# A column of ones beside V, attention ahead of the fold, and 384 columns a matmul

## The chip, the cores and the metric

The kernel runs on one core of a Trainium2 chip. Its engines are TensorE (PE; PEld is its weight load), VectorE (DVE), ScalarE (ACT), GpSimd (POOL) and SyncE (SP, which here issues every DMA). Each has its own queue of instructions, in order. The metric is device time in microseconds (us) of one execution, as the median of several runs.

## What is computed

A random-feature attention, a gated layer with two products behind it, and four experts that all work on every token:

```
q, k, v: 2 batches x 8 heads x 576 tokens x 64
phi(x) = exp(x omega' - |x|^2/2 - max) / sqrt(128)        # 128 features a token
kv = k'^T v ;  z = sum over tokens of k'
attn = (q' kv) / (q' z + 1e-6)                            # per head
x = attn as 1152 tokens x 512
h = ((x w1) * (x w2)) w3 w_out                            # 512 -> 1024 -> 1024 -> 512
out = sum over e of p_e * relu(h ew1_e) ew2_e             # 4 experts, 512 -> 1024 -> 512
```

w1, w2, w3 and w_out come as float64, the rest as float32. Products after the attention are made of operands that are each the sum of two float32r numbers (a high and a low part, made by `split`), in three passes: low by high, high by low, high by high.

## The kernel before

**Tokens.** Each batch has 576 tokens, 512 main ones (4 x 128) and a tail of 64. The tails of both batches share one tile of 128 rows. A *pair* is two heads of one batch; there are eight pairs. x stands transposed in `xt`, with one set of four tiles for each batch.

**The attention of a pair** (lines 261 to 365). `load` fetches k, q and v of 512 tokens. `transpose_kq` turns k and q on TensorE. `features` (L215) makes 4 x 128 projections in one PSUM bank, VectorE takes their maximum (L227), ScalarE makes four exponentials (L229). `sum_k` adds K' over tokens on GpSimd (L298 to L300), `kv_sums` (L309) makes (K'V)^T of both heads at once, `kv_place` (L315 and L316) turns it back and spreads the sums of K' with a matmul of ones. `normalise` (L333 to L338) multiplies each row of Q' by the sums on VectorE, adds it up, inverts it, and GpSimd scales Q'. `transpose_e` (L348) turns Q' and `attend` (L363) makes 288 columns of x at a time. A pair is spread over three steps of a loop.

**Float64 weights.** `from_f64` (L75 to L86) loads a block of 128 x 512 numbers (512 KB) into one of two tiles and makes float32 of it with one ScalarE and three VectorE instructions (L83, L84, L85). `split` (L69, L70) then takes ScalarE for the high and, for w1, w2 and w_out, GpSimd for the low part. There are 48 such blocks: 16 of w1 and w2, of which 8 are converted a second time, 8 of w_out, 16 of w3.

**The middle.** `gated` makes 128 rows of (x w1) * (x w2) for one batch in two pieces of 288 columns (L147). `fold` makes w3 w_out: four transposes of a w3 block (into ps_w and ps_x by turns), a split, 12 matmuls of 512 columns (L174), twice for each of eight rows; the sums stand in ps_po and ps_et by turns. `expert_input` multiplies the two for one batch (L192).

**The experts.** For each, eight groups of first-layer columns in four pieces of 288 (L474) and nine token tiles of 512 columns (L493). Their raw weights go through `raw_p`, four tiles that exist from the start.

**The order.** A scheduler orders the instructions of each engine by priority. Table `BESIDE` says what stands beside each attention step (conversions and the first six gated rows of batch 0), `AFTER` what follows. Attention steps run with a priority shift of -100.

## Time and profile before

| | |
|---|---|
| median of 3 runs | 733.59 us (733.46 to 733.74) |
| the profiled execution, first to last instruction | 732.2 us |
| TensorE busy | 700.5 us, 96% |
| VectorE busy | 345.6 us, 47% |
| ScalarE busy | 241.0 us, 33% |
| GpSimd busy | 100.7 us, 14% |

The span leaves out some 1.4 us that lie around the first and last instruction. The page cuts the span into 40 slices; "busy" for TensorE means that some matmul is in flight, not that the engine is at its peak. Shares are averages over stages: the attention fills roughly the first 165 us, the fold follows to about 238, then the other products, and from 329 us on the experts run, 100.17 us each.

### The profile page before, as it was taken

Reading aid. Unit: us, or ns where it says so; the run is one execution under the profiler, and the core shown is the slowest. Engines: PE = TensorE matmul, PEld = TensorE weight load, DVE = VectorE, ACT = ScalarE, POOL = GpSimd, SP = SyncE. Lnnn points to the kernel's source line nnn. Section 1 sums busy time; section 2 is a strip of 40 time slices with the busy share of each in tenths; the row PEclk is TensorE's granted clock in tenths of the full one; section 3 lists DMA queues with packets and bytes.
Section 4 is the critical chain, followed back from the end, with each engine's and each line's share of the span. In section 5 each row is a group of like instructions: output and inputs, shape, how many; then the busy total and the mean of one; then the engine's idle time right before and its main releaser. Section 6 shows DMA issues by size and latency. Waiting matters only on the chain.

```text
span 732.2 us, 10963 instructions
## 1 busy us (share of the span) xinstructions
PE 700.5 (96%) x4353; PEld 625.6 (85%) x4353; DVE 345.6 (47%) x752; ACT 241.0 (33%) x602; POOL 100.7 (14%) x114
## 2 busy tenths in 40 slices
PE   6997887889999999999999999999999999999997
PEld 4765667778888999999998899988899988999886
DVE  3799999997766275612431154231334311422111
ACT  4777766464332254512330033210223200322000
POOL 1557664450000041000000000000000000000000
PEclk9999998999999999999999999999999999999999
DMA  6526322453443021500110031010211100100011
GB/s 175 174 77 198 116 86 88 144 173 126 133 144 116 1 87 44 162 26 2 58 59 0 1 116 56 3 58 0 71 46 59 59 1 0 58 1 1 30 49 52
DMA packets 37858, 52.13 MB, mean 71 GB/s; under 512 B 6960, under 2 KB 25392, under 8 KB 37808
## 3 DMA queue, kind: packets, MB, share of 16 engines
q1 hardware_dynamic: 37808, 51.44, 22.8%
q8 instruction: 34, 0.56, 0.3%
q14 instruction: 16, 0.13, 0.1%
HBM read 49.07 MB, written 2.36 MB: 70 GB/s over the span
## 4 chain that ended last, share of the span: by engine, by line
PE 80%; DVE 14%; DMA 2%; ACT 2%; issue 1%; SPq 0%; POOL 0%; DVEq 0%; ACTq 0%
PE ps_f L493 7%; PE ps_f L474 7%; PE ps_et L493 4%; PE ps_kv L493 4%; PE ps_t L474 3%; PE ps_w L474 3%; PE ps_kv L474 3%; PE ps_po L474 3%; PE ps_x L474 3%; PE ps_et L474 3%; PE ps_et L174 3%; DVE t L333 3%; PE ps_t L493 3%; PE ps_w L493 3%; PE ps_x L493 3%; PE ps_po L493 3%
## 5 line engine op out<-in xcount | busy, mean ns | idle before, releaser
L474 PE MATMUL ps_f<-x,w 128*128 128x288 f32 x384 | 102.7, 295 | 0.0
L474 PEld LDWEIGHTS ps_f<-x,w 128*128 128x128 f32 x384 | 72.3, 188 | 0.1
L69 ACT ACTIVATE w<-w2r 128x512 fp32r<-128x512 f32 x32 | 20.2, 632 | 140.1 <-PE ps_f L493 44.5
L147 PE MATMUL ps_w<-xt,w 128*128 128x288 f32 x240 | 49.3, 309 | 8.7 <-ACT a L154 3.4
L493 PE MATMUL ps_f<-w,hid 128*128 128x512 f32 x240 | 56.1, 389 | 0.0
L493 PEld LDWEIGHTS ps_f<-w,hid 128*128 128x128 f32 x240 | 44.9, 188 | 9.2
L147 PE MATMUL ps_po<-xt,w 128*128 128x288 f32 x240 | 48.5, 307 | 4.0 <-DVE a L158 3.1
L474 PE MATMUL ps_w<-x,w 128*128 128x288 f32 x192 | 51.4, 295 | 0.0
L474 PE MATMUL ps_t<-x,w 128*128 128x288 f32 x192 | 51.4, 295 | 0.0
L474 PE MATMUL ps_kv<-x,w 128*128 128x288 f32 x192 | 51.4, 295 | 0.0
L474 PE MATMUL ps_po<-x,w 128*128 128x288 f32 x192 | 51.4, 295 | 0.0
L474 PE MATMUL ps_x<-x,w 128*128 128x288 f32 x192 | 51.4, 295 | 0.0
L474 PE MATMUL ps_et<-x,w 128*128 128x288 f32 x192 | 51.3, 295 | 0.0
L70 POOL TENSOR_TENSOR w<-w12f,w 128x512 fp32r<-128x512 f32 x24 | 33.4, 1394 | 120.3 <-ACT w L69 112.9
L147 PEld LDWEIGHTS ps_w<-xt,w 128*128 128x128 f32 x240 | 38.7, 195 | 11.7 <-ACT a L154 3.7
L147 PEld LDWEIGHTS ps_po<-xt,w 128*128 128x128 f32 x240 | 38.7, 195 | 5.7 <-DVE a L158 3.6
L83 DVE TENSOR_SCALAR f64e<-f 128x512 uint32<-128x512 uint32 x48 | 27.0, 567 | 24.8 <-DMA f<-in_moe_w_dram 23.8
L84 DVE SCALAR_TENSOR_TENSOR f64e<-f,f64e 128x512 uint32<-128x512 uint32 x48 | 38.4, 803 | 0.5
L474 PEld LDWEIGHTS ps_kv<-x,w 128*128 128x128 f32 x192 | 36.2, 189 | 0.0
L474 PEld LDWEIGHTS ps_w<-x,w 128*128 128x128 f32 x192 | 36.2, 189 | 0.0
L474 PEld LDWEIGHTS ps_t<-x,w 128*128 128x128 f32 x192 | 36.2, 189 | 0.0
L474 PEld LDWEIGHTS ps_et<-x,w 128*128 128x128 f32 x192 | 36.1, 188 | 0.1
(194 smaller groups left out, 1472.2 us busy)
## 6 DMA issues: line engine op xcount, KB each, us to landing
f<-in_moe_w_dram SPq DMA_DIRECT2D x40, 512.0 KB, 3.7
w1r<-in_moe_w_dram SPq DMA_DIRECT2D x32, 256.0 KB, 3.0
w2r<-in_moe_w_dram SPq DMA_DIRECT2D x32, 256.0 KB, 2.8
f<-in_moe_w_out_dram SPq DMA_DIRECT2D x8, 512.0 KB, 3.6
kr<-in_k_dram SPq DMA_DIRECT2D x8, 256.0 KB, 2.8
vr<-in_v_dram SPq DMA_DIRECT2D x8, 256.0 KB, 3.7
qr<-in_q_dram SPq DMA_DIRECT2D x8, 256.0 KB, 2.8
out_dram<-acc SPq DMA_DIRECT2D x8, 256.0 KB, 2.1
```

The lines of the kernel that those rows point to most:

```text
L69: nc.scalar.activation(out=hi, in_=src, func=ACTF.Copy)
L70: (eng or nc.vector).tensor_tensor(out=lo, in0=src, in1=hi.bitcast(F32), op=ALU.subtract)
L83: nc.vector.tensor_scalar(out=e, in0=high, scalar1=0x80000000, scalar2=None, op0=ALU.bitwise_and)
L84: nc.vector.scalar_tensor_tensor(out=e, in0=low, scalar=29, in1=e, op0=ALU.logical_shift_right, op1=ALU.bitwise_or)
L147: nc.tensor.matmul(out=bs[c][:, :HS], lhsT=w12[w, g][:, x, kk], rhs=xt[b][kk][:, y, c * HS:(c + 1) * HS], start=(kk == 0 and n == 0), stop ...
L174: nc.tensor.matmul(out=po, lhsT=wt[:, a, g * P:(g + 1) * P], rhs=wo[hf * 4 + g][:, c], start=(n == 0), stop=(n == 3 * KF - 1),)
L333: nc.vector.scalar_tensor_tensor(out=t, in0=e[:, g], scalar=1.0, in1=zs[g], op0=ALU.mult, op1=ALU.mult, accum_out=d[:, g],)
L474: nc.tensor.matmul(out=banks[2 * b + c][:, :HS], lhsT=w1t[kk][:, x, g * P:(g + 1) * P], rhs=x2[b, kk][:, y, c * HS:(c + 1) * HS], start=(k ...
L493: nc.tensor.matmul(out=ps, lhsT=hd[f][:, x, t * P:(t + 1) * P], rhs=w2t[f][:, y], start=(n == 0), stop=(n == 3 * KE - 1),)
```

## The change

- V stands in tiles of 65 columns a head, `va`, with a column of ones at the end. The product K'V (L320 of the new kernel) then has the sums of K' as its 65th column, and Q' times that has the denominator beside the numerator. `normalised` inverts and multiplies 256 numbers a head, not Q'. `sum_k`, `kv_place` and `normalise` are gone. The product comes with tokens in rows, and `place` turns it.
- Q' is made by one subtraction of all four maxima on VectorE and one exponential (`wide`).
- The tails of Q' are turned once at the start, and `attend_tail` does the tails of a batch behind its last pair.
- A pair takes two steps. The attention has a priority shift of 100000. Beside it stand the conversion of w_out and the fold; the tables are gone. The fold has one bank for transposes and one for sums, and two w3T tiles.
- All low halves of converted weights are made by VectorE. Every block is converted once: 40 in all.
- `gated`, `expert_input` and the experts' first layer work on all 1152 tokens in three pieces of 384 columns (`columns`), over eight banks in turn.
- `raw_p` opens after the gated stage.

```diff
-BESIDE = {
-    3: "w0 w1", 4: "w2", 5: "b00 w3 o", 6: "b01 w4 o", 7: "b02 w5 o", 8: "b03 w6 o", 9: "b04 w7 b05 o",
-}
-AFTER = "b06 b07 o o o f0 f1 f2 f3 f4 f5 f6 f7 c0 b14 b15 b16 b17 w0 b10 w1 b11 w2 b12 w3 b13 c1"
...
+ATTENTION_FIRST = 100000
...
-    HS = S // 2
+    CH = NT // 3
...
-    xt_p = ctx.enter_context(tc.tile_pool(name="xt", bufs=2 * KD))
-    w1_p = ctx.enter_context(tc.tile_pool(name="w1", bufs=8))
-    raw_p = ctx.enter_context(tc.tile_pool(name="raw", bufs=4))
+    xt_p = ctx.enter_context(tc.tile_pool(name="xt", bufs=KD))
+    w1_p = ctx.enter_context(tc.tile_pool(name="w1", bufs=10))
...
+    def next_bank():
+        turn[0] += 1
+        return bank(("t", "f", "kv", "et", "f", "x", "w", "po")[turn[0] % 8])
...
-        f = cv.tile([P, 512], F32, tag="f64f", name=name, bufs=3)
+        f = cv.tile([P, 512], F32, tag="f64f", name=name, bufs=2)
...
-    xt = [[xt_p.tile([P, 2, S], F32R, tag="xt", name=f"xt{i}") for i in range(NPAIR)] for _ in range(B)]
...
+    xt = [xt_p.tile([P, 2, NT], F32R, tag="xt", name=f"xt{i}") for i in range(NPAIR)]
...
-    wo_p = mctx.enter_context(tc.tile_pool(name="wo", bufs=KF))
-    h_p = mctx.enter_context(tc.tile_pool(name="h", bufs=KF))
...
+    w3_p = mctx.enter_context(tc.tile_pool(name="w3", bufs=1))
...
-            t = load_w64(w1_p, src, "w12", nc.gpsimd)
...
-        wo.append(load_w64(wo_p, mwo[f * P:(f + 1) * P].unsqueeze(1), "wo", nc.gpsimd))
...
-    def fold(w3_p, m):
...
-        po = bank(("po", "et")[m % 2])
...
+            t = load_w64(w1_p, src[:, g * P:(g + 1) * P].rearrange("(k p) c -> p k c", p=P), "w12", nc.vector)
...
+        wo.append(load_w64(w1_p, mwo[f * P:(f + 1) * P].unsqueeze(1), "wo", nc.vector))
...
+    def fold(m):
...
+        po = bank("po")
...
-            ps = bank(("w", "x")[hf])
+            ps = bank("w")
...
-            wt = w3_p.tile([P, 2, 512], F32R, tag="w3T", name="w3T", bufs=3)
+            wt = w3_p.tile([P, 2, 512], F32R, tag="w3T", name="w3T", bufs=2)
...
+    def columns(lhsT, rhs, nk):
...
+        bs = [next_bank() for _ in range(NT // CH)]
+        for kk in range(nk):
+            for n, (x, y) in enumerate(PASSES):
+                for c, ps in enumerate(bs):
+                    nc.tensor.matmul(
+                        out=ps[:, :CH], lhsT=lhsT(kk, x), rhs=rhs[kk][:, y, c * CH:(c + 1) * CH],
+                        start=(kk == 0 and n == 0), stop=(kk == nk - 1 and n == 2),
+                    )
+        return [(ps[:, :CH], slice(c * CH, (c + 1) * CH)) for c, ps in enumerate(bs)]
...
+    def gated(a_p, h_p, g):
...
+        ws = load_w12(g)
+        ht = h_p.tile([P, 2, NT], F32R, tag="h", name="hid")
+        parts = []
+        for w in range(2):
+            for c, (ps, s) in enumerate(columns(lambda kk, x: ws[w][:, x, kk], xt, KD)):
+                if w == 0:
+                    t = a_p.tile([P, CH], F32, tag="a", name="a", bufs=6)
+                    nc.scalar.activation(out=t, in_=ps, func=ACTF.Copy)
+                    parts.append(t)
+                else:
+                    t = parts[c]
+                    nc.vector.tensor_tensor(out=t, in0=ps, in1=t, op=ALU.mult)
+                    split(ht[:, HI, s], ht[:, LO, s], t)
+        hid.append(ht)
...
+    def expert_input():
         for j in range(KD):
...
+            t = xt_p.tile([P, 2, NT], F32R, tag="xt", name="x2")
+            for ps, s in columns(lambda kk, x: w3o[kk][:, x, j * P:(j + 1) * P], hid, KF):
+                split(t[:, HI, s], t[:, LO, s], ps)
+            x2.append(t)
...
-            for g in range(4):
-                last = nc.scalar.activation(out=e[:, g], in_=pv[:, g], func=ACTF.Exp, bias=mx[:, g:g + 1])
+            if wide:
+                nc.vector.tensor_tensor(out=e, in0=pv, in1=mx.unsqueeze(2).to_broadcast([P, 4, M]), op=ALU.add)
+                last = nc.scalar.activation(out=e, in_=e, func=ACTF.Exp)
+            else:
+                for g in range(4):
+                    last = nc.scalar.activation(out=e[:, g], in_=pv[:, g], func=ACTF.Exp, bias=mx[:, g:g + 1])
...
+        va = [st.tile([P, 2 * R, D1], F32, name=f"va{n}") for n in range(3)]
+        for t in va:
+            nc.gpsimd.memset(t[:, :, D:], 1.0)
...
-        eqt = st.tile([P, H, M], F32, name="eqt")
+        eTt = st.tile([P, H, P], F32, name="eTt")
...
+            m, t = (0, MAIN) if b == 0 else (S + TAIL, S)
+            return slice(m, m + MAIN), slice(t, t + TAIL)
...
+        def normalised(out, ps, rows, n):
...
+            v = ps[rows, :n * D1].rearrange("p (n d) -> p n d", d=D1)
+            d = at.tile([P, 4], F32, tag="d", name="d", bufs=4)[rows, :n]
+            nc.vector.tensor_scalar(out=d, in0=v[:, :, D], scalar1=EPS, scalar2=None, op0=ALU.add)
+            nc.vector.reciprocal(out=d, in_=d)
+            nc.vector.tensor_tensor(
+                out=out, in0=v[:, :, :D], in1=d.unsqueeze(2).to_broadcast(list(out.shape)), op=ALU.mult,
+            )
...
+                self.va = va[self.n % 3]
...
-                for name, src, bufs in (("kr", k, 1), ("qr", q, 1), ("vr", v, 2)):
...
+                for h in range(2):
+                    nc.sync.dma_start(
+                        out=self.va[:, h * R:(h + 1) * R, :D], in_=v[b, 2 * i + h, :MAIN, :].rearrange("(p r) d -> p r d", r=R),
+                    )
...
+                self.eq[j] = at.tile([P, R, M], F32, tag="eq", name="eq", bufs=3)
+                self.mark = features(self.qT, j, self.eq[j], wide=True)
...
                 ps = bank("kv")
...
+                for j in range(2):
+                    h = 2 * self.i + j
+                    for r in range(R + 1):
+                        e, a = (self.ek[j][:, r], self.va[:, j * R + r]) if r < R else (ekt[:, h], vt[self.b][:, h])
+                        nc.tensor.matmul(out=ps[:, j * D1:(j + 1) * D1], lhsT=e, rhs=a, start=(r == 0), stop=(r == R))
+                self.kva = at.tile([P, 2, D1], F32, tag="kva", name="kva", bufs=NPAIR + 1)
+                nc.scalar.activation(out=self.kva, in_=ps[:, :2 * D1].rearrange("p (j d) -> p j d", j=2), func=ACTF.Copy)
...
+                self.eT[j] = at.tile([P, MAIN], F32, tag="eT", name="eT", bufs=2)
+                for r in range(R):
+                    transpose(ps[:, r * P:(r + 1) * P], self.eq[j][:, r])
+                nc.scalar.activation(out=self.eT[j], in_=ps, func=ACTF.Copy)
...
+            def attend(self):
+                self.xs = at.tile([P, R, 2, D], F32, tag="xs", name="xs")
+                for j in range(2):
+                    ps = bank(("x", "kv")[j])
                     for r in range(R):
...
+                        nc.tensor.matmul(
+                            out=ps[:, r * D1:(r + 1) * D1], lhsT=self.eT[j][:, r * P:(r + 1) * P], rhs=self.kva[:, j],
+                            start=True, stop=True,
                         )
...
+                    normalised(self.xs[:, :, j], ps, slice(0, P), R)
...
+            def place(self):
+                ps = bank("et")
+                for r in range(R):
+                    transpose(ps[:, r * P:(r + 1) * P], self.xs[:, r].rearrange("p j d -> p (j d)"))
+                x, s = xt[self.i], cols(self.b)[0]
+                split(x[:, HI, s], x[:, LO, s], ps)
...
+        def attend_tail(b, ps_of):
...
+            rows = rows_of[b]
+            xs = at.tile([P, H, D], F32, tag="xs", name="xs")
+            for f in range(2):
+                ps = bank(("x", "kv")[f])
+                for g in range(4):
+                    h = f * 4 + g
+                    nc.tensor.matmul(
+                        out=ps[rows, g * D1:(g + 1) * D1], lhsT=eTt[:, h, rows], rhs=ps_of[h // 2].kva[:, h % 2],
+                        start=True, stop=True,
+                    )
+                normalised(xs[rows, f * 4:(f + 1) * 4], ps, rows, 4)
...
-        for n in range(len(pairs) + 2):
-            u, u1, u2, nx = pair(n), pair(n - 1), pair(n - 2), pair(n + 1)
-            with tc.high_priority(offset=-100):
...
+        for n in range(len(pairs) + 1):
+            u, u1, nx = pair(n), pair(n - 1), pair(n + 1)
+            with tc.high_priority(offset=ATTENTION_FIRST):
...
-                if u:
-                    for j in range(2):
-                        u.features_k(j)
-                        u.sum_k(j)
                 if u1:
                     u1.kv_sums()
-                if u2:
-                    for j in range(3):
-                        u2.transpose_e(j)
+                if u:
+                    u.features_k(0)
+                    u.features_k(1)
+                if u1:
+                    u1.transpose_e(0)
+                    u1.transpose_e(1)
                 if u:
                     u.features_q(0)
+                    u.features_q(1)
                 if u1:
-                    u1.kv_place()
-                if u:
-                    u.features_q(1)
-                if u2:
-                    u2.attend(0)
-                    u2.attend(1)
-                if u1:
-                    for j in range(3):
-                        u1.normalise(j)
+                    u1.attend()
                 if nx:
                     nx.transpose_kq()
...
+                if u1:
+                    u1.place()
+                    if u1.i == NPAIR - 1:
+                        attend_tail(u1.b, pairs[u1.n - u1.i:u1.n + 1])
+        for f in range(KF):
+            load_wo(f)
+        for m in range(KF):
+            fold(m)
...
-    for s in AFTER.split():
...
+    h_p = mctx.enter_context(tc.tile_pool(name="h", bufs=KF, reuse_waits="tile"))
+    a_p = mctx.enter_context(tc.tile_pool(name="a", bufs=1, reuse_waits="tile"))
+    for g in range(KF):
+        gated(a_p, h_p, g)
+    expert_input()
...
+    raw_p = ctx.enter_context(tc.tile_pool(name="raw", bufs=4, reuse_waits="tile"))
...
+                for ps, s in columns(lambda kk, x: w1t[kk][:, x, g * P:(g + 1) * P], x2, KD):
+                    nc.scalar.activation(out=ht[:, HI, s], in_=ps, func=ACTF.Relu)
                     nc.vector.scalar_tensor_tensor(
-                        out=ht[:, LO, s], in0=banks[c][:, :HS], scalar=0.0, in1=ht[:, HI, s].bitcast(F32),
-                        op0=ALU.max, op1=ALU.subtract,
+                        out=ht[:, LO, s], in0=ps, scalar=0.0, in1=ht[:, HI, s].bitcast(F32), op0=ALU.max, op1=ALU.subtract,
                     )
```

How the queues move is seen at three places. First SP at the start, where `kr` and `qr` at L233 (L229 after) are the tails of k and q, and `va` is V. Before:

```order
L233 DMA kr<-in_k_dram 64x8x64 x2
L245 DMA om_raw<-in_omega_dram 128x64
L233 DMA qr<-in_q_dram 64x8x64 x2
L233 DMA vt_117<-in_v_dram 64x8x64
L233 DMA vt_120<-in_v_dram 64x8x64
L274 DMA kr<-in_k_dram 128x2x256
```

After:

```order
L298 DMA va_108<-in_v_dram 128x4x64
L298 DMA va_109<-in_v_dram 128x4x64 x2
L298 DMA va_108<-in_v_dram 128x4x64
L229 DMA kr<-in_k_dram 64x8x64 x2
L242 DMA om_raw<-in_omega_dram 128x64
L229 DMA qr<-in_q_dram 64x8x64 x2
L229 DMA vt_113<-in_v_dram 64x8x64
```

Four loads of V, of the second and third pair, moved ahead of the first tails.

Second VectorE in the middle of the attention. Before, about the third pair (`t,d<-eq,z` is the product with the sums of K'):

```order
L333 SCALAR_TENSOR_TENSOR t,d<-eq,z 128x128 x2
L85 SCALAR_TENSOR_TENSOR w12f<-w12f,f64e 128x512
L84 SCALAR_TENSOR_TENSOR f64e<-f_862,f64e 128x512
L333 SCALAR_TENSOR_TENSOR t,d<-eq,z 128x128
L227 TENSOR_REDUCE mx<-ps_f 128x4
L210 TENSOR_SCALAR kT<-ps_t 128x512
L333 SCALAR_TENSOR_TENSOR t,d<-eq,z 128x128
L70 TENSOR_TENSOR xt_84<-ps_x,xt_84 128x288
```

After, between two rounds of the fold (`w3T` is the split of the transposed w3 block, `w3f` and `f64e` belong to the conversion of the next blocks):

```order
L63 TENSOR_TENSOR w3T<-ps_w,w3T 128x512
L78 SCALAR_TENSOR_TENSOR w3f<-w3f,f64e 128x512
L219 TENSOR_REDUCE mx<-ps_f 128x4
L202 TENSOR_SCALAR kT<-ps_t 128x512
L76 TENSOR_SCALAR f64e<-f_1420 128x512
L77 SCALAR_TENSOR_TENSOR f64e<-f_1420,f64e 128x512
L63 TENSOR_TENSOR w3o<-ps_po,w3o 128x512
L63 TENSOR_TENSOR w3T<-ps_w,w3T 128x512
```

The products are gone, and the fold's conversions and splits stand in their place. In this order the first split w3T is VectorE's 81st row, the last its 232nd; the last piece of `xt` is written by its 296th.

Third TensorE near the end of the attention. Before, the last attention matmuls (L363) stand among gated ones of batch 0:

```order
L147 MATMUL ps_kv<-xt_84,w_1840 128x288
L147 MATMUL ps_t<-xt_85,w_1840 128x288
L363 MATMUL ps_x<-eT,kv 64x288 x2
L147 MATMUL ps_kv<-xt_85,w_1840 128x288
L147 MATMUL ps_t<-xt_85,w_1840 128x288
```

After, the K'V sums of the last pair (L320):

```order
L159 MATMUL ps_f<-xt_80,w_1732 128x384
L159 MATMUL ps_w<-xt_80,w_1732 128x384
L159 MATMUL ps_f<-xt_81,w_1732 128x384
L320 MATMUL ps_kv<-va_108,ek 128x65 x4
L320 MATMUL ps_kv<-vt_117,ekt 128x65
L320 MATMUL ps_kv<-va_108,ek 128x65 x4
L320 MATMUL ps_kv<-vt_117,ekt 128x65
L92 MATMUL ps_et<-ident,xs 128x128 x4
L159 MATMUL ps_f<-xt_81,w_1732 128x384 x2
```

Gated matmuls stand ahead of the last pair here too, 72 of the 576 before the last piece of x is placed.

## Rows read from the trace of the kernel before

**Rows 1.** The page: span, and busy time (share, instructions) by engine.

```profile
span 732.2 us, 10963 instructions
PE 700.5 (96%) x4353; PEld 625.6 (85%) x4353; DVE 345.6 (47%) x752; ACT 241.0 (33%) x602; POOL 100.7 (14%) x114
```

**Rows 2.** Stretches: busy us (x instructions) of five engines, clock, DMA share, GB/s.

```profile
0.00:10.00 10.00, 4.11 (x14) 3.41 (x15) 1.37 (x4) 1.88 (x2) 2.09 (x10) 1.00 0.61 151
10.00:20.00 10.00, 8.73 (x38) 6.66 (x37) 5.44 (x8) 7.17 (x25) 0.80 (x2) 1.00 0.74 196
...
30.00:165.00 135.00, 116.38 (x748) 90.77 (x746) 129.82 (x345) 88.99 (x249) 81.02 (x86) 0.97 0.41 126
```

**Rows 3.** The chain that ended last, in order of time: start, us, what.

```profile
316.09 3.20 PE ps_x L192 x24
...
378.81 5.47 PE ps_f L493 x24
384.28 5.44 PE ps_kv L493 x24
...
478.98 5.46 PE ps_kv L493 x24
...
728.33 0.75 DVE acc L501
```

**Rows 4.** VectorE by line (total, mean ns): three from 100 us, four from 165.

```profile
L85 DVE SCALAR_TENSOR_TENSOR wof<-wof,f64e 128x512 uint32<-128x512 uint32 x7 | 8.9, 1266 | 0.2
L333 DVE SCALAR_TENSOR_TENSOR t<-eq,z 128x128 bf16<-128x128 f32 x16 | 5.5, 375 | 0.0
L70 DVE TENSOR_TENSOR xt<-ps_x,xt 128x288 fp32r<-128x288 f32 x6 | 2.7, 448 | 0.0
...
L84 DVE SCALAR_TENSOR_TENSOR f64e<-f,f64e 128x512 uint32<-128x512 uint32 x19 | 13.1, 687 | 0.3
L85 DVE SCALAR_TENSOR_TENSOR w3f<-w3f,f64e 128x512 uint32<-128x512 uint32 x15 | 10.3, 684 | 0.1
L83 DVE TENSOR_SCALAR f64e<-f 128x512 uint32<-128x512 uint32 x19 | 8.1, 428 | 20.9 <-DMA f<-in_moe_w_dram 20.8
L70 DVE TENSOR_TENSOR w3T<-ps_w,w3T 128x512 fp32r<-128x512 f32 x8 | 5.5, 686 | 0.3 <-ACT w3T L69 0.3
```

**Rows 5.** VectorE in order of time: start, us, line, operation.

```profile
64.34 0.68 DVE L85 SCALAR_TENSOR_TENSOR w12f<-w12f,f64e 128x512 uint32<-128x512 uint32 x1
64.94 0.16 DVE L336 TENSOR_SCALAR d<-d 128x4 f32<-128x4 f32 x1
...
65.90 0.68 DVE L227 TENSOR_REDUCE mx<-ps_f 128x4 f32<-128x512 f32 x1
```

**Rows 6.** SP's queue at the start, in order of time.

```profile
0.74 1.44 SPq L233 DMA_DIRECT2D kr<-in_k_dram  x2
...
4.21 1.31 SPq L233 DMA_DIRECT2D vt<-in_v_dram  x2
```

**Rows 7.** The fold: chain, four transposes, both halves of a split.

```profile
183.24 3.04 PE ps_et L174 x12
...
188.17 2.74 PE ps_et L174 x12
191.47 2.75 PE ps_po L174 x12
...
126.56 0.66 PE L99 MATMUL ps_et<-ident,eq 128*128 128x128 f32 x4
...
186.75 0.60 ACT L69 ACTIVATE w3T<-ps_w 128x512 fp32r<-128x512 f32 x1 [2.51 <-PE ps_w L99]
...
187.38 0.69 DVE L70 TENSOR_TENSOR w3T<-ps_w,w3T 128x512 fp32r<-128x512 f32 x1 [0.26 <-ACT w3T L69]
```

**Rows 8.** A stretch, and TensorE in order of time, about 120 us.

```profile
120.00:130.00 10.00, 10.00 (x54) 9.34 (x55) 9.18 (x20) 7.37 (x17) 3.52 (x3) 0.71 0.52 159
...
119.97 3.25 PE L147 MATMUL ps_w<-xt,w 128*128 128x288 f32 x12 [3.44 <-ACT a L154]
```

More of the change, by code (lines that the diff above doesn't have):

```diff
@@ L127, in load_w12 @@
+    hid, wo, w3o, x2 = [], [], [], []
     def load_w12(g):
[L129 to L159 removed]
@@ L201, in attention_moe_kernel @@
         st = actx.enter_context(tc.tile_pool(name="st", bufs=1))
+        D1 = D + 1
         def transposed(r, name, tag="t"):
@@ L213, in transposed, with features @@
             return t
-        def features(t, half, e, tag="f"):
+        def features(t, half, e, tag="f", wide=False):
             ps = bank(tag)
@@ L358, in attend @@
-            def attend(self, c):
-                ps = bank("x")
-                s = slice(c * HS, (c + 1) * HS)
-                for j in range(2):
-                    h = slice(j * D, (j + 1) * D)
-                    nc.tensor.matmul(out=ps[h, :HS], lhsT=self.kv[:, h], rhs=self.eT[j][:, s], start=True, stop=True)
-                x = xt[self.b][self.i]
-                split(x[:, HI, s], x[:, LO, s], ps[:, :HS])
+                for j in range(2):
[3 more added lines that the diff above has]
+                        nc.tensor.matmul(out=ps[:, j * D1:(j + 1) * D1], lhsT=e, rhs=a, start=(r == 0), stop=(r == R))
@@ new lines, in place @@
+            def place(self):
+                ps = bank("et")
+                for r in range(R):
+                    transpose(ps[:, r * P:(r + 1) * P], self.xs[:, r].rearrange("p j d -> p (j d)"))
[11 more added lines that the diff above has]
+                        start=True, stop=True,
+                    )
+                normalised(xs[rows, f * 4:(f + 1) * 4], ps, rows, 4)
+            ps = bank("et")
+            s = cols(b)[1]
+            for i in range(NPAIR):
+                transpose(ps[:, i * TAIL:(i + 1) * TAIL], xs[rows, 2 * i:2 * i + 2].rearrange("p j d -> p (j d)"), rows)
+            for i in range(NPAIR):
+                x = xt[i]
+                split(x[:, HI, s], x[:, LO, s], ps[:, i * TAIL:(i + 1) * TAIL])
@@ L377, in attention_moe_kernel @@
         for half in range(2):
-            features(qT, half, eqt[:, half * 4:half * 4 + 4], ("w", "po")[half])
-        for n in range(len(pairs) + 2):
-            u, u1, u2, nx = pair(n), pair(n - 1), pair(n - 2), pair(n + 1)
-            with tc.high_priority(offset=-100):
+            e = at.tile([P, R, M], F32, tag="eq", name="eq", bufs=3)
+            features(qT, half, e, ("w", "po")[half])
+            ps = bank("x")
+            for g in range(4):
+                transpose(ps[:, g * P:(g + 1) * P], e[:, g])
@@ L401, in attention_moe_kernel @@
-                if u2:
-                    u2.attend(0)
-                    u2.attend(1)
-                if u1:
-                    for j in range(3):
-                        u1.normalise(j)
+                    u1.attend()
                 if nx:
                     nx.transpose_kq()
-            with ExitStack() as order:
-                for ins in u.mark if u else ():
-                    order.enter_context(tc.issue_after(ins))
-                for s in BESIDE.get(n, "").split():
-                    if s[0] == "w":
-                        load_w12(int(s[1]))
-                    elif s[0] == "o":
-                        load_wo()
-                    else:
-                        gated(at, 2, int(s[1]), int(s[2]), ("w", "po") * 2)
```

148 lines of the change are left out of this document (16 added, 132 removed).

## The prediction

> **What bounds the kernel now.** I read the page first. TensorE is busy for 700.5 of 732.2 us [rows 1], an average over stages: where it is full only its own work counts, elsewhere something else may set the pace. The cut into stretches shows where: from 30 to 165 us VectorE is busy for 129.8 of 135 us, TensorE for 116.4 and ScalarE for 89.0 [rows 2]. The attention stage is bound by VectorE. The first 20 us are a start-up in which VectorE works for 1.37 + 5.44 = 6.8 us, so it idles for 13.2 [rows 2].
>
> From about 170 us on the chain runs on TensorE alone. Its price per matmul is read from groups of 24: 3.20 us for 288 columns, 5.44 us for 512, that is 133.3 and 226.7 ns [rows 3]. The difference, 93.3 ns for 224 columns, is 0.4167 ns a column (2.4 GHz); what is left is 13.3 ns a matmul at either size. One expert takes 478.98 - 378.81 = 100.17 us: 384 matmuls of 288 (51.2) and 216 of 512 (48.97). VectorE takes the last sum at 728.33, and the span ends 3.9 us later.
>
> **Columns: 384 in place of 288.** The same columns go through in three pieces, not four. A matmul of 384 costs 160 + 13.3 = 173.3 ns. There are 672 matmuls fewer (192 in the gated product, 96 in the expert input, 384 in the experts' first layer), so 672 x 13.3 ns = 9.0 us leave a path that has nothing beside it. New stage times: gated 576 x 173.3 = 99.8 us (102.4 before), expert input 288 x 173.3 = 49.9 (51.2), four experts 4 x (49.92 + 48.97) = 395.6 (400.7). ScalarE and VectorE evacuate as many elements in fewer instructions, under matmuls: nothing.
>
> The Trainium skill, page "TensorE: Matmul & The Clock Gate", section "Wait — 56ns, not 53.3ns?", puts the warm spacing at the columns over 2.4 GHz plus about 2.5 ns. By that the 672 matmuls would save 1.7 us and the time would be 7 us later than I forecast. The trace disagrees with it for these operands, 133.3 ns where the rule makes 122.5.
>
> **What is late until the last attention column is placed.** Call that moment T. After it only TensorE's matmuls follow. The orders show that 72 of the 576 gated matmuls stand ahead of it, so 504 x 173.3 = 87.4 us follow, then 49.9, 395.6 and the end's 3.9: 536.8 us in all. The span is T + 536.8. So T decides, and it stands where VectorE has done its instructions 1 to 296 of the new order.
>
> **VectorE up to T, part by part.** Removed: 64 products with the sums of K' (375 ns each [rows 4]) with their small followers, and 8 of the 48 float64 blocks (w1 and w2 are converted once, not one and a half times). Added: 16 wide subtractions from PSUM (as the split from PSUM, 686 ns), the normalisation of 256 numbers twice a pair (between 0.16 us for a tiny one [rows 5] and 0.448 for 288 numbers [rows 4], 0.42 as nearest to the latter), and the low half of the split of the converted blocks, which was GpSimd's. GpSimd, 100.7 us busy before [rows 1], has nothing left but memsets. What that does for VectorE is in the rows: the same last conversion step takes 1266 ns on a w_out block while GpSimd works and 684 on a w3 block when it doesn't [rows 4]. I therefore price all steps as in the undisturbed stretch: 428, 687 and 684 ns for a block's three steps, 686 for a split [rows 4], 0.68 us for a maximum [rows 5].
>
> The sum: 185 instructions of 512 elements (9 kT, 36 maxima, 16 wide ones, 38 + 36 conversion steps, 50 splits) at 0.684 is 126.5; 38 first steps at 0.428 is 16.3; 20 normalisations at 0.2 + 0.17 + 0.42 is 15.8; small ones 4.5. That is 163 us at full durations. But an instruction that needs nothing from the one ahead starts before that one's end: a step of 0.68 us at 64.34 is followed at 64.94, 0.08 us early [rows 5]. I take this for 200 of the 295 (the others wait for their neighbour, as a block's second step does): 16 us, so 147. All 295 would make 140, none 163.
>
> ScalarE loses 48 of the 64 exponential instructions on Q and gains little; at 89.0 of 135 us before it stays below VectorE. TensorE up to T has the attention, the fold and 72 gated matmuls, in sum below VectorE's.
>
> **The start.** Four loads of V in 256-byte pieces now stand ahead of the first K tail on SP's queue; SP issues wait in line behind them. Two tail loads of V, in pieces of the same size, took 1.31 us to issue [rows 6], so four take 2.6 us and start-up idling becomes 13.2 + 2.6 = 15.8. If their data also hold up K, another 1 us; if not needed in time, nothing.
>
> **VectorE's idling after the start.** Before, 5.2 of 135 us [rows 2], with work always in reserve. Now the fold goes beside the attention through one bank ps_w, one bank ps_po and two w3f buffers: its 16 rounds are a ring. One round is 12 matmuls (2.74), four transposes (0.66), ScalarE's half of the split (0.60), VectorE's (0.69) [rows 7]: 4.7 us, 5.0 with the hops between engines. VectorE's own work between the first and the last of them in the new order is 4.9 us a round. So neither hides the other wholly; each round waits behind attention instructions on three engines. I take 5.7 us a round: 15 x 0.8 = 12 us idle, and 3 us elsewhere. The bounds are 5.0 (1.5 us idle) and 6.5 (24).
>
> **The sum.** T = 15.8 + 147 + 15 = 177.8. Span 177.8 + 536.8 = 714.6 us against 732.2. The median of the runs lies 1.4 us above the profiled span, so 716.0 us, 2.4% less.
>
> **What the clock may add.** The granted clock is 1.00 nearly throughout; after TensorE idled 3.44 us it stood at 0.71 for the ten us from 120, and a group of 12 that takes 1.6 us at the full clock started at 119.97 and took 3.25 [rows 8]. With a lighter load on TensorE such a gap near T costs 3 us; earlier ones hide under VectorE.
>
> **Prefetch and buffers.** raw_p now opens after the gated stage and takes over memory of the conversion tiles, so the first expert weights come later; they are needed 87 + 50 us after T, and loads and splits of them stand in the gated stage of the order: nothing. If that cover failed it would cost one landing of some 3 us. The w1 pool of ten tiles holds eight of w_out and two of w12; the others follow as the fold ends, in its shade.
>
> **Rivals.** (a) The fold's ring becomes the bound. Between two splits of w3T the new order has only some 4 to 12 VectorE instructions, and TensorE's 12 matmuls must come before the next transposes. With rounds of 7.5 us the idling is 3 + 15 x 2.6 = 42: T = 205, time 743. It decides from T = 195.3 (7.0 us with 0.2% on top), that is rounds of 6.9. For it: single banks, in-order queues, and a gated group that waits for converted weights ahead of the last pair's K'V sums. Against: in the fold of before a round with nothing else in its way took 4.93 and 3.30 us by turns [rows 7].
> (b) Nothing overlaps on VectorE: 163, T = 193.8, time 732, no change. The row of 0.60 us spacing speaks against it [rows 5]. The Trainium skill, page "VectorE: DVE Perf Modes", section "The DRAIN you can't avoid", says that a next instruction doesn't start until the pipe is empty; that would be this case, and the trace shows 0.08 us less.
> (c) The ring costs nothing and all 295 overlap: 15.8 + 140 + 4.5 = 160.3, time 698.5. It needs engines that never meet.
> (d) The change doesn't do what it says: attention is not alone with the fold, since the order puts ten converted w1/w2 blocks and 72 gated matmuls ahead of its end. That is in my sum already; were it otherwise, T would be some 20 us earlier and the gated stage as much longer.
>
> **How the numbers follow.** Forecast, rounds of 5.0 to 6.5 us and overlaps between 143 and 151: 0.77. (a) 0.11, (b) 0.06, (c) 0.06. The low end is 15.8 + 143 + 4.5 = 163.3, 701.5 us. The high end has 24 + 3 idle, 3 for the clock and 148 of work: T = 193.8, 732, which I cut to 731, where (b) begins. A comparison can tell about 0.2%, 1.5 us. Faster: 0.77 + 0.06 + half of (b) = 0.86; same 0.03; slower 0.11.
>
> **What would show it.** Right: experts 98.9 us apart, groups of 36 matmuls in 6.24 us; VectorE 90% busy from 30 us to T, its conversion steps at 684 whatever the block; T near 178. Wrong: w3T waits of several us on TensorE's queue with VectorE idle (a); 512-element steps spaced by 0.68 (b); half clock after T; or the first maximum later than about 13 us.

## The result

The changed kernel takes 741.36 us (median of 4 runs, 739.37 to 742.27) against 733.54 (733.46 to 733.74) for the one before: a ratio of 1.0099, 95% interval 1.0087 to 1.0111. It is 1.0% slower; the forecast was 716.0 with a range to 731.0. The profiled execution has a span of 739.7 us, forecast 714.6.

The page of after answers to [rows 1]: TensorE 700.5 to 703.6 us, VectorE 345.6 to 298.7, GpSimd 100.7 to 2.4. The last row is the granted clock in 40 slices, in tenths (9 is 90% or more).

```profile
span 739.7 us, 9257 instructions
PE 703.6 (95%) x3785; PEld 645.3 (87%) x3785; DVE 298.7 (40%) x568; ACT 210.5 (28%) x456; POOL 2.4 (0%) x15
...
PEclk9979999999599999999999999999999999999999
```

What stands behind the attention went as forecast. In the chain that ended last, one expert's second layer starts at 389.63 and the next expert's at 488.58: 98.95 us apart (98.9 forecast; 100.17 before [rows 3]).

```profile
389.63 4.80 PE ps_x L464 x21
...
488.58 4.80 PE ps_w L464 x21
...
735.51 0.75 DVE acc L472
```

The last piece of x is in place at 202.6 us, when VectorE's last split of xt ends (202.38 + 0.23). From there to the end are 537.1 us, forecast 536.8. So all of the error is in T: 202.6 for 177.8.

```profile
202.38 0.23 DVE L63 TENSOR_TENSOR xt<-ps_et,xt 128x64 fp32r<-128x64 f32 x1 [0.29 <-ACT xt L62]
```

### The profile page after: what moved, and what is told of

Same layout as the page of the kernel before. It is cut to its first block, busy times and chain, and to the rows that moved or that the text cites. A ratio compares the mean times of both kernels' runs of the same rounds, so it can differ in the third digit from the quotient of the medians.

```text
span 739.7 us, 9257 instructions
## 1 busy us (share of the span) xinstructions
PE 703.6 (95%) x3785; PEld 645.3 (87%) x3785; DVE 298.7 (40%) x568; ACT 210.5 (28%) x456; POOL 2.4 (0%) x15
## 4 chain that ended last, share of the span: by engine, by line
PE 85%; DMA 6%; DVE 5%; ACT 3%; SPq 1%; issue 0%; DVEq 0%; ACTq 0%
PE ps_f L159 11%; PE ps_kv L159 6%; PE ps_et L159 6%; PE ps_f L464 6%; PE ps_x L159 6%; PE ps_t L159 6%; PE ps_w L159 5%; PE ps_po L159 5%; DMA f<-in_moe_w_dram 5%; PE ps_po L144 5%; PE ps_t L464 4%; PE ps_po L464 4%; PE ps_x L464 4%; PE ps_w L464 4%; PE ps_et L464 3%; PE ps_kv L464 3%
## 5 line engine op out<-in xcount | busy, mean ns | idle before, releaser
L159 PE MATMUL ps_f<-x,w 128*128 128x384 f32 x288 | 96.2, 334 | 0.0
L144 PE MATMUL ps_po<-wo,w3T 128*128 128x512 f32 x192 | 49.4, 402 | 2.0 <-DVE w3T L63 2.0
L159 PE MATMUL ps_t<-x,w 128*128 128x384 f32 x144 | 48.1, 334 | 0.0
L159 PE MATMUL ps_po<-x,w 128*128 128x384 f32 x144 | 48.1, 334 | 0.0
L159 PE MATMUL ps_kv<-x,w 128*128 128x384 f32 x144 | 48.1, 334 | 0.0
L159 PE MATMUL ps_w<-x,w 128*128 128x384 f32 x144 | 48.1, 334 | 0.0
L159 PE MATMUL ps_x<-x,w 128*128 128x384 f32 x144 | 48.1, 334 | 0.0
L159 PE MATMUL ps_et<-x,w 128*128 128x384 f32 x144 | 48.1, 334 | 0.0
L159 PE MATMUL ps_f<-xt,w 128*128 128x384 f32 x144 | 44.6, 344 | 0.0
L144 PEld LDWEIGHTS ps_po<-wo,w3T 128*128 128x128 f32 x192 | 34.9, 188 | 9.1 <-DVE w3T L63 2.4
```

Of the source, the lines that this page charges most:

```text
L144: nc.tensor.matmul(out=po, lhsT=wt[:, a, g * P:(g + 1) * P], rhs=wo[hf * 4 + g][:, c], start=(n == 0), stop=(n == 3 * KF - 1),)
L159: nc.tensor.matmul(out=ps[:, :CH], lhsT=lhsT(kk, x), rhs=rhs[kk][:, y, c * CH:(c + 1) * CH], start=(kk == 0 and n == 0), stop=(kk == nk - ...
```

## The profile after, by stage

First the kernel before, then after, each cut at 20, 60 and 165 us; columns as in [rows 2].

```profile
0.00:20.00 20.00, 12.85 (x51) 10.07 (x51) 6.81 (x12) 9.05 (x27) 2.90 (x12) 1.00 0.67 174
20.00:60.00 40.00, 39.05 (x248) 27.26 (x246) 34.51 (x120) 29.71 (x98) 24.42 (x36) 1.00 0.45 143
60.00:165.00 105.00, 86.81 (x569) 70.23 (x569) 101.86 (x242) 65.64 (x176) 61.68 (x59) 0.97 0.42 127
165.00:220.00 55.00, 53.45 (x311) 46.35 (x312) 38.23 (x71) 21.50 (x42) 0.00 (x0) 1.00 0.43 134
```

```profile
0.00:20.00 20.00, 11.53 (x49) 9.05 (x49) 8.10 (x16) 8.68 (x23) 2.45 (x15) 1.00 0.65 175
20.00:60.00 40.00, 31.63 (x172) 26.42 (x173) 36.56 (x75) 27.05 (x63) 0.00 (x0) 0.87 0.69 210
60.00:165.00 105.00, 97.97 (x600) 84.45 (x598) 70.98 (x145) 49.07 (x112) 0.00 (x0) 0.98 0.30 92
165.00:202.90 37.90, 29.94 (x168) 26.96 (x168) 30.34 (x66) 16.54 (x32) 0.00 (x0) 0.79 0.47 149
0.00:202.90 202.90, 171.06 (x985) 146.88 (x986) 145.98 (x300) 101.33 (x228) 2.45 (x15) 0.93 0.45 134
...
165.00:220.00 55.00, 47.04 (x263) 44.06 (x263) 39.78 (x85) 25.14 (x50) 0.00 (x0) 0.84 0.38 122
```

Two things have changed places. From 60 to 165 us VectorE was the full engine (101.9 of 105 us); now it is TensorE (98.0 of 105), and VectorE is busy for 71.0. And from 20 to 60 us TensorE, which had 39.1 us of work, now has 31.6, at a granted clock of 0.87. (The cut at 202.9 lies 0.3 us behind T.)

Hence an account of the span by the engine that ends last. I cut the trace into slices of 5 us: TensorE's idle time is the slice less its busy time; "half clock" is the busy time times what the granted clock is short of 1.00; the rest is work at full clock. The last column gives idle time by stretch; the 3.9 and 4.2 us that it leaves out lie behind 220 us.

| kernel | span | work | idle | half clock | idle: 0-20, 20-60, 60-165, 165-220 |
|---|---|---|---|---|---|
| before | 732.2 | 697.4 | 31.8 | 3.0 | 7.2, 0.9, 18.2, 1.5 |
| after | 739.7 | 691.8 | 36.1 | 11.9 | 8.5, 8.4, 7.0, 8.0 |

TensorE's work fell by 5.6 us. If the columns gave their 9.0, everything else that changed adds 3.4 (a difference; I didn't take it apart). Idle time rose by 4.3 and half clock by 8.9: 7.5 us slower in all.

Three places stand out. **The start:** with four loads of V ahead on SP's queue the first maximum comes at 12.34 us, 10.02 before. VectorE's rows, before and after:

```profile
10.02 0.69 DVE L227 TENSOR_REDUCE mx<-ps_f 128x4 f32<-128x512 f32 x1 [2.73 <-PE ps_f L221]
...
12.34 0.69 DVE L219 TENSOR_REDUCE mx<-ps_f 128x4 f32<-128x512 f32 x1 [2.45 <-PE ps_f L213]
```

**The landings:** a view of the waits up to 215 us shows VectorE idle for 24.8 us until float64 blocks land (total us, times, longest). On SP's queue their loads wait for a free staging tile, the tile that a block lands in, of which there are two.

```profile
DVE f64e L76 <- DMA f<-in_moe_w_dram: 24.8, 22, 4.1
...
SPq L69 <- ACT w3f L75: 62.5, 13, 8.4
SPq L69 <- DVE f64e L77: 39.8, 18, 4.4
SPq L69 <- ACT w12f L75: 31.4, 5, 19.9
```

**The last pair:** its normalisation (L273 to L275) stands in VectorE's queue between conversions of w1 and w2, some of which wait for such landings (4.1 us of idle time from 165 to 204 us). In order of time on VectorE, with the idle time and its releaser in brackets:

```profile
186.09 0.43 DVE L76 TENSOR_SCALAR f64e<-f 128x512 uint32<-128x512 uint32 x1 [0.56 <-DMA f<-in_moe_w_dram]
186.44 0.15 DVE L273 TENSOR_SCALAR d<-ps_x 128x4 f32<-128x4 f32 x1
...
187.64 0.43 DVE L76 TENSOR_SCALAR f64e<-f 128x512 uint32<-128x512 uint32 x1 [0.31 <-DMA f<-in_moe_w_dram]
...
188.66 0.41 DVE L275 TENSOR_TENSOR xs<-ps_x,d 128x256 f32<-128x256 f32 x1
...
191.17 0.42 DVE L275 TENSOR_TENSOR xs<-ps_kv,d 128x256 f32<-128x256 f32 x1
...
196.27 0.69 DVE L63 TENSOR_TENSOR xt<-ps_et,xt 128x512 fp32r<-128x512 f32 x1
```

From `d` to the split of xt are 9.8 us, of which these steps of the pair work for under 3; most of the rest is the conversions' own work. TensorE waits with them, at a granted clock down to 0.50.

## Experiments

Each is an edit of the changed kernel ("after"), or of the combined version ("All together", below). Ratios are to the kernel before on the same chip, with 95% intervals; after itself stands at 1.0099, and versions are compared with it through these ratios. The versions scatter by up to 1.3% from run to run where the kernel before scatters by 0.3 to 0.6%, so a gain under 2 us is not read from them. T is read from the one profiled execution of a version. That of after is the slowest of its four runs (742.27 us), that of three staging tiles the fastest of ten (732.25), so differences of T can be some 3 us larger than those of the medians.

### Three staging tiles

```
-        r = cv.tile([P, 512, 2], U32, tag="f64", name="f64", bufs=2)
+        r = cv.tile([P, 512, 2], U32, tag="f64", name="f64", bufs=3)
```

> Three staging tiles for float64 blocks in place of two, nothing else. Staging theory: the loads wait for a staging tile (62.5 us of waits on SP's queue for ScalarE's conversion step), so the blocks land late and VectorE, which works in order, stands 51 us on their landing; with a third tile at least half of that goes, and T falls by 12 us or more: 729 us or less. TensorE theory: from 60 to 165 us TensorE is busy for 98.0 of 105 us, so VectorE's waits there cost nothing, and only waits at the end of the attention can go: 735 to 741 us.

734.91 us, ratio 1.0008 (0.9985 to 1.0031): 0.9% faster than after. VectorE's wait for landings is gone, and T came to 193.2:

```profile
DVE f64e L76 <- DMA f<-in_moe_w_dram: 2.0, 2, 1.2
```

So the staging tiles did cause the wait of 24.8 us (not 51, as the expectation has it), but its going gave only 6 to 7 us, at the edge of what the TensorE theory allowed. VectorE does as much work up to T as before (145.3 us); in part it now waits for other engines instead, 9.7 us for the projections (6.7 in after) and 9.0 for ScalarE's half of w3o (1.3).

### A third of the fold's matmuls

```
-                for a, c in PASSES:
+                for a, c in PASSES[2:]:
```

> The fold leaves out two of its three products of high and low halves (64 matmuls of 512 columns remain of 192); conversions, transposes, splits and transfers are all there. TensorE theory: 128 matmuls at 226.7 ns, 29 us, leave a TensorE that is full from 60 to 165 us, and T falls by 18 to 29 us: 712 to 723 us, with VectorE nearly full in that stretch. Staging theory: the float64 blocks come no sooner, so T stays within 5 us: 736 to 741 us, with TensorE idle in the room that was made.

731.63 us, 0.9964 (0.9940 to 0.9988): some 10 us faster than after, where matmuls priced at 29 us were taken out. Both theories missed. By the account TensorE's work fell by 24.9 us (to 666.9), while its idle time rose by 7.2 (to 43.3) and half clock by 8.6 (to 20.5). The first row is after's fold matmuls with their first and last start, the second this kernel's: sixteen rounds end 43 us sooner, so it was largely TensorE's matmuls that set their pace. T came only to 195.3. The third row, a stretch, shows what came in their place: with w_out's blocks released, twelve conversions of w1 and w2 went ahead between the last pairs' steps, and VectorE was full, 36.7 of 40 us.

```profile
L144 PE MATMUL ps_po<-wo,w3T x192: 387/389/587, 57.3 to 170.0; 128*128 128x512 f32 x192
```

```profile
L144 PE MATMUL ps_po<-wo,w3T x64: 387/397/774, 55.5 to 126.6; 128*128 128x512 f32 x64
...
120.00:160.00 40.00, 27.16 (x136) 22.62 (x134) 36.66 (x76) 24.37 (x50) 0.00 (x0) 0.84 0.54 158
```

### A shorter conversion on VectorE

```
-        nc.vector.tensor_scalar(out=e, in0=high, scalar1=0x80000000, scalar2=None, op0=ALU.bitwise_and)
-        nc.vector.scalar_tensor_tensor(out=e, in0=low, scalar=29, in1=e, ...)
+        nc.vector.scalar_tensor_tensor(out=e, in0=low, scalar=29, in1=high, ...)
```

> The changed kernel without the first of VectorE's three steps on each float64 block (the one that keeps the sign), so the converted weights are not the reference's; 38 instructions of 0.428 us, 16.3 us, leave VectorE ahead of T. If VectorE's work sets T, as the prediction had it, the time falls by about 16 us to 725. By the account (TensorE's work at full clock, plus its idle time, plus half clock) VectorE binds only from 20 to 60 us, where some ten of the blocks are converted: 4 to 5 us less, 736 to 738.

735.09 us, 1.0005 (0.9986 to 1.0024): 6 to 7 us faster than after, T at 197.0. Of 16.3 us of VectorE's work less than half came back, so VectorE's work alone does not set T. It is also somewhat more than the 4 to 5 us that the account gave for the stretch from 20 to 60 us, by a margin close to the intervals.

### The conversions of w1 and w2 behind the attention

```
...
+    with tc.issue_after(placed):      # the last split of xt, on VectorE
         for g in range(KF):
             gated(a_p, h_p, g)
```

> The conversions of w1 and w2 stand behind the last attention instruction in VectorE's queue, and with them all 576 matmuls of the gated product; nothing else changes. Queue theory: with no conversion that waits for a landing between the last pairs' attention steps, T comes some 8 us after the fold's end at 170, at 178; then about 6 us until the first w1 block is converted, and 99.8 + 49.9 + 395.6 + 4 = 549 us of matmuls: 733 us. If the last pairs are late for another reason, T stays near 200: 755 us.

745.45 us, 1.0156 (1.0141 to 1.0172). T came to 187.4, 15 us sooner than in after. The edit takes two things away from the last pair, and the run alone doesn't tell them apart: the conversions in VectorE's queue, and in TensorE's queue the gated matmuls ahead of T. In after 63 of these (10.9 us at 173.3 ns) stand between the matmuls of the last two pairs, from 165 to 182 us, and TensorE works through them without a pause. Below are after's transposes of Q' for the last pair; then this kernel's, and its first normalising step.

```profile
180.66 0.60 PE L92 MATMUL ps_et<-ident,eq 128*128 128x128 f32 x4
```

```profile
173.29 0.74 PE L92 MATMUL ps_et<-ident,eq 128*128 128x128 f32 x4 [1.41 <-DVE xt L63]
...
177.54 0.16 DVE L273 TENSOR_SCALAR d<-ps_x 128x4 f32<-128x4 f32 x1 [4.30 <-PE ps_x L336]
```

The pair's `d` comes at 177.54 for 186.44: 8.9 us are won ahead of it, most of them where the gated matmuls stood. From `d` to T are 9.8 us for 16.2: these 6.4 us lie where after's TensorE waits and its VectorE converts. So the rows speak for the conversions in 6 of the 15 us and for the gated matmuls in most of the other 9; no run moves one without the other. And it was given back: all 576 gated matmuls now follow T, and TensorE stands until the first converted block, as these rows of TensorE in order of time show.

```profile
184.44 0.84 PE L92 MATMUL ps_et<-ident,xs 64*128 64x64 f32 x4 [1.28 <-DVE xt L63]
191.26 0.69 PE L159 MATMUL ps_f<-xt,w 128*128 128x384 f32 x1 [5.98 <-DVE w L63]
```

T was 9 us later than the queue theory said.

### V's loads behind the tails'

```
+                with tc.issue_after(tails):    # the last tail load on SP's queue
                     for h in range(2):
                         nc.sync.dma_start(out=self.va[...], in_=v[...])
```

> The loads of V of a pair are issued behind the loads of the tails instead of ahead of them. The first maximum then comes near 10.0 us as in the kernel before, not at 13.6. If what follows is a chain of work, the time falls by the same 3.6 us, to 738 us. If the attention stage is paced by blocks landing later on, it stays at 741 us.

736.09 us, 1.0026 (1.0005 to 1.0046): 0.7% faster than after; the first maximum stands at 9.74 us in the chain, 2.6 us sooner. (The 13.6 of the expectation is after's second maximum, so its 3.6 us are too many.) The start does carry through to T (196.2), by more than its own 2.6 us; the order of the next steps changed with it, so the rest isn't attributed.

```profile
8.17 1.54 PE ps_f L213 x4
9.74 0.70 DVE mx L219
```

### Both together

Three staging tiles and V's loads behind the tails'.

> Three staging tiles and V's loads behind the tails' loads, together. By an account of the span as TensorE's work at full clock (692 us) plus its idle time plus what half clock costs, the two edits take away 2 us of idle at the start, 3 to 4 of the waits from 20 to 165 us, and 3 us of half clock: 728 to 731 us, less than either alone (734.9 and 736.1). If both worked by the same waits, the time stays at 734 us.

729.91 us, 0.9936 (0.9917 to 0.9954). The two gains add up, 12 us below after and 0.6% below the kernel before.

### A pool of its own for w_out

```
-        wo.append(load_w64(w1_p, mwo[f * P:(f + 1) * P].unsqueeze(1), "wo", nc.vector))
+        wo.append(load_w64(wo_p, mwo[f * P:(f + 1) * P].unsqueeze(1), "wo", nc.vector))
...
+        wo_p = actx.enter_context(tc.tile_pool(name="wo", bufs=KF))
```

> The eight blocks of w_out get a pool of their own in memory that is free during the attention, so that w1 and w2 can be converted while the fold still runs and not only when its w_out blocks are free; still two staging tiles. Queue theory: the last pair's normalisation no longer stands behind conversions that wait for a landing (18 us of such landings on the chain from 165 us on), TensorE idles less than 4 us after 165 us and keeps its clock: 732 us or less. Staging theory: the landings are as late as before, only earlier in the order, and the time stays within 3 us of 741.4.

740.55 us, 1.0078 (1.0063 to 1.0094): no change that can be told from after. VectorE still waits 21.8 us for landings (24.8 in after): with two staging tiles the blocks land about as late as before, whatever memory waits for them behind. The queue theory's 732 is out.

### All together

The same pool, eight tiles for w1 and w2, four staging tiles, V's loads behind the tails'.

> All together: w_out's own pool, eight tiles for w1 and w2, four staging tiles, V's loads behind the tails' loads. By the account (692 us of work at full clock): idle 6.4 at the start, 7 from 20 to 60, 4 from 60 to 165, 3 after it, 4 at the end, and 4 us of half clock: 720 us, faster than both kernels. If the attention's own chain from pair to pair sets the pace, idle and half clock stay as with three staging tiles: 731 us.

722.68 us (721.35 to 723.84), 0.9839 (0.9821 to 0.9856): 1.6% faster than the kernel before, 2.6% faster than after. T is 185.0. By the same stretches:

```profile
0.00:20.00 20.00, 13.63 (x58) 11.11 (x59) 8.44 (x17) 9.31 (x27) 2.45 (x15) 1.00 0.76 221
20.00:60.00 40.00, 32.06 (x196) 26.79 (x195) 38.38 (x82) 26.99 (x61) 0.00 (x0) 0.96 0.69 213
60.00:165.00 105.00, 101.07 (x625) 88.17 (x624) 78.23 (x160) 54.62 (x121) 0.00 (x0) 1.00 0.37 115
165.00:220.00 55.00, 52.75 (x318) 51.26 (x317) 34.62 (x74) 22.86 (x48) 0.00 (x0) 0.97 0.25 79
```

By the account: work 693.1, idle 24.6, half clock 2.6, span 720.4. The work is within 1.3 us of after's; all of the gain is idle time (11.5 us) and half clock (9.3).

### Columns in four pieces again

`CH = NT // 4` in place of `NT // 3`, once in the changed kernel, once in the combined one. With it the tiles `a` of the gated stage, which are smaller now, are five and not six.

> Four pieces of 288 columns again in place of three of 384, in the gated product, the expert input and the experts' first layer; all else as changed. By the price of 13.3 ns for every matmul there are 672 more, 9.0 us: 750.4 us, experts 100.2 us apart. If a matmul's fixed part were nearly nothing here, the time would stay within 2 us of 741.4.

> The combined version with four pieces of 288 columns in place of three of 384. Its TensorE waits little ahead of the gated stage, so the price of the columns should show whole: 672 x 13.3 ns = 9.0 us more, 731.7 us. If part of what 384 columns save is given back as waits, less than 5 us more.

In the combined one: 732.01 us, 0.9971 (0.9960 to 0.9982), 9.3 us more (9.7 by the ratios, with an interval of some 1.5 either way). That agrees with the term: 13.9 ns for each of the 672 matmuls, for 13.3 read from [rows 3]. In the changed kernel: 746.04 us (737.60 to 747.35 in six runs), 1.0163 (1.0143 to 1.0183), only 4.7 more than after. Its runs scatter by more than the term, and its profiled execution (span 735.8) is far from its median, so its time tells nothing of the columns. Its trace does, for the experts: their second layers start 100.17 us apart, 1.22 more than in after, as forecast.

```profile
382.44 4.79 PE ps_f L464 x21
...
482.61 4.78 PE ps_kv L464 x21
```

In its gated product and expert input, though, a matmul of 288 columns comes every 130.0 ns, for 133.3 in the combined version with four pieces and 173.3 for 384 columns in after. At 130.0 four pieces cost what three of 384 do. The same stretch, first here, then in the combined version with four pieces; the number in the first brackets is TensorE's matmuls:

```profile
210.00:250.00 40.00, 40.00 (x310) 40.00 (x309) 14.93 (x34) 12.50 (x32) 0.00 (x0) 1.00 0.15 47
```

```profile
210.00:250.00 40.00, 40.00 (x303) 40.00 (x302) 15.10 (x36) 13.13 (x34) 0.00 (x0) 1.00 0.13 41
```

Why the two differ is open; the fixed 13.3 ns of the term are thus not the same in every stage. The gated matmuls that start ahead of T are not the reason for the small difference: 107 of 768 here and 79 of 576 in after, some 14 us of work in both.

### Two buffers for K and Q

`def raw_tile(name, bufs=2)` in the combined version.

> The combined version with two buffers each for a pair's K and Q. In it the chain stood 5.42 us on the landing of one pair's K at 26 us, issued only when the one buffer was free; 7.9 us of TensorE's idle time lie from 20 to 60 us. If the late issue is the cause, 3 to 5 us of them go: 718 to 720 us. If VectorE, busy 38.4 of those 40 us, is the cause, it stays at 722 to 723.

723.99 us, 0.9881 (0.9842 to 0.9921): no gain. TensorE's wait of 3.0 us for that K is gone, and in the two stretches from 20 to 60 us VectorE is full as before; the late K was not the cause.

```profile
20.00:40.00 20.00, 16.43 (x76) 12.07 (x76) 19.38 (x43) 14.67 (x32) 0.00 (x0) 0.84 0.75 237
40.00:60.00 20.00, 16.55 (x107) 13.93 (x105) 20.00 (x42) 12.08 (x27) 0.00 (x0) 0.99 0.69 211
```

### Useless matmuls in the last gaps

```
+        def filler(k, last):
+            with tc.issue_after(last.ins):
+                ps = bank("t")
+                for _ in range(k):
+                    nc.tensor.matmul(out=ps[:, :256], lhsT=ident, rhs=om..., start=True, stop=True)
...
+                    if self.n == B * NPAIR - 1:
+                        filler((5, 12)[j], last)
...
+                if b and f:
+                    filler(6, last)
```

> The changed kernel with 23 matmuls of 256 columns of constants (their results are not used, some 5 us at full clock) put into TensorE's queue where it waits for the last pair's normalisation and the tail's, from 183 to 197 us. There the granted clock was 0.50 to 0.85, and half clock cost 5.8 us from 165 us on. If it is the idle gaps that bring the clock down, it stays near 1.00 there and 3 to 5 us go: 736 to 738 us. If the clock falls all the same, the time stays at 741 us or rises by up to 3 us, since the added matmuls stand in the way of the tail's.

740.80 us, 1.0113 (1.0066 to 1.0161): not to be told from after. First after, then this kernel, by stretches:

```profile
180.00:190.00 10.00, 5.71 (x42) 5.10 (x41) 8.61 (x20) 5.55 (x10) 0.00 (x0) 0.85 0.48 161
190.00:200.00 10.00, 6.64 (x28) 4.95 (x27) 7.46 (x17) 1.28 (x2) 0.00 (x0) 0.50 0.41 128
```

```profile
180.00:190.00 10.00, 10.00 (x60) 8.97 (x59) 8.19 (x18) 4.91 (x8) 0.00 (x0) 1.00 0.49 160
190.00:200.00 10.00, 8.47 (x53) 6.65 (x51) 6.64 (x17) 1.46 (x4) 0.00 (x0) 1.00 0.32 105
```

The clock holds at 1.00 when the gaps are filled, so the gaps brought it down. (The 23 matmuls took 10.6 us by the account, not the 5 that I expected.) Yet T moved by 0.4 us (202.2): from 183 us on the last pair waits for VectorE's queue, not for TensorE. Half clock there was a symptom. The profiled span is 2.1 us shorter (737.6), which the scatter of the runs doesn't let one tell from nothing.

## Why the prediction was wrong

**What held.** The columns' term (9.0 us; 9.3 measured in the combined version), experts 98.9 us apart, 536.8 us after T (537.1; that it is so near is luck in part, since 79 and not 72 gated matmuls started ahead of T, and the granted clock was still 0.68 up to 205 us), VectorE's work up to T (147 us; 146.0), its conversion steps at 0.67 to 0.69 us whatever the block with GpSimd at rest. The rule of the Trainium skill that the prediction weighed, page "TensorE: Matmul & The Clock Gate", section "Wait — 56ns, not 53.3ns?" (about 2.5 ns beside the columns), would have made 1.7 us of the 9.3. Rival (b), no overlap on VectorE, is out: the 300 instructions up to T last 161.9 us in all, and 196 of them start before the one ahead ends, by 15.9 us in sum (16 forecast, for 200). The section of the Trainium skill named there, page "VectorE: DVE Perf Modes", section "The DRAIN you can't avoid", adds that a next instruction that isn't held starts earlier, so it doesn't stand against these 196 as the prediction had it.

**The step that failed** is the term "VectorE's idling after the start", 15 us, and ahead of it the sentence that TensorE's work up to T is "in sum below VectorE's". That sum was never made. TensorE's work at full clock is 691.8 us, and 532.9 of it follow T (536.8 less the end's 3.9): 158.9 us stand ahead of T, more than VectorE's 146. VectorE's idle time up to 202.9 us is 11.9 in the first 20 us (15.8 forecast for the start), 3.4 to 60, 34.0 to 165 and 7.6 after it: 45.0 where the term said 15. VectorE was 75% busy from 30 us to T, where 90% was named as the sign. The missing sum doesn't explain all of it: 158.9 and TensorE's 8.5 us of idle time at the start make 167.4, still below the 177.8 of the forecast. The remaining 35 us are TensorE's idle time behind the first 20 us (23.4) and half clock (11.9).

The size of a fold round shows it. I took 5.7 us from the ring's own links, with bounds of 5.0 and 6.5. The first round's matmuls start at 57.3 and the sixteenth's at 167.44: 7.34 us a round.

```profile
167.44 2.92 PE L144 MATMUL ps_po<-wo,w3T 128*128 128x512 f32 x12
```

TensorE is busy for 98.0 of 105 us there, 6.85 a round. By their tiles the fold's matmuls and transposes are 53.8 us of that, 3.8 a round, and the rest, 3.1, is nearly all attention. The bounds had VectorE's own work in a round (4.9 us) and left TensorE's attention out; with it, and TensorE as busy as here, a round is 6.85 on average at the least.

**Rival (a)** named that size, rounds of 7.5, T 205, 743 us, with a chance of 0.11; 7.34, 202.6 and 741.4 came. Its sign, waits for w3T on TensorE's queue, is nearly absent: 2.0 us of idle time ahead of the fold's matmuls.

```profile
L144 PE MATMUL ps_po<-wo,w3T 128*128 128x512 f32 x192 | 49.4, 402 | 2.0 <-DVE w3T L63 2.0
```

So the size came by another way, and that rival (a) met it is luck: not a ring that waits for its own links, but a TensorE that is full from 60 to 165 us, with the queues and the landings around it. One of its reasons did come, gated matmuls ahead of the last pair's K'V sums; they waited for nothing, but their work stood in the way.

**"The others follow as the fold ends, in its shade"** was the second miss. The conversions of w1 and w2 there wait for landings (two staging tiles; the waits for them were in the row of 20.9 us that I had read only for its durations [rows 4]), and in VectorE's in-order queue they held the last pair up, while the gated matmuls that they feed did the same in TensorE's: T at 187.4 with both behind it, at 202.6 with both between. The rows put 6.4 us behind the pair's first step on VectorE and 8.9 ahead of it; how much of the 8.9 is TensorE's queue alone was not tried.

**The start** was right in kind: 2.3 us later (12.34 for 10.02), 2.6 forecast; and it counts, as its removal gave 5 us. But the term was VectorE's idling, 15.8 us, and that came to 11.9, less than the 13.2 of before.

**The clock** stood in the high end with 3 us and not in the sum. Half clock came to 11.9 us by the account, 4.6 of it from 20 to 60 us and 5.8 from 165 on; filling the last gaps showed that it costs little where TensorE waits anyway.

**No single bound.** Taking 29 us from TensorE gave 10, 16 from VectorE gave 6 to 7, 23 of waiting for landings gave 6 to 7. The two engines have 159 and 146 us of work for a stage of 203 and hand each step to each other in fixed order. That a relief of one is therefore soon taken up by the other is my reading of the rows; no run isolates it. What paid was to take away the waits of both: 18.7 us for the combined version. What sets its remaining 24.6 us of idle time is open.

## What to carry to other kernels

When a change takes work from the engine that binds a stage, sum the work of every engine up to the same moment, not only the one that bound before: the next engine's sum is the least that the stage can take, and waits come on top. A conversion or a load put ahead of a critical step in an in-order queue brings all of its waits with it, and so does the work that it feeds, in the next engine's queue; count the staging tiles behind it and price its landing where the step stands. An account of the span as the last engine's work, idle time and half clock shows in one line where a gain went, but the three are not independent: half clock inside a wait cost nothing here that could be measured.

## What the hardware showed that I had not expected

Useless work in TensorE's gaps held its granted clock at 1.00 where it had been 0.85 and 0.50, without a gain in time that could be measured. The same matmul of 288 columns came every 130.0 ns in one kernel and every 133.3 in another. And the versions scatter more than the kernel before: 732.25 to 739.77 us in ten runs with three staging tiles, 733.16 to 737.21 in twenty-five of the kernel before beside them. Why was not tried, in either case.
